# A gated linear recurrence and a SoLU feed-forward on one core: running sums in tiles of 32 columns, a ScalarE test in place of clamps, a carried phase on 16 rows, and a newly written order

## The chip, the core and the metric

The kernel runs on one core of a Trainium2 chip. The metric is the device time of one execution in microseconds. The engines are TensorE (PE; its weight loads are listed apart as PEld), VectorE (DVE), ScalarE (ACT), GpSimd (POOL) and SyncE (SP, which issues nearly all DMAs here).

## The reference, cut to what matters

For each of 4 batches and 8 heads a 48x48 complex state is decayed channel by channel and updated over 768 steps. The output of this part is the input of a feed-forward with 384 inputs and 1024 hidden units, over 3072 tokens.

```python
mag = np.sqrt(a_re * a_re + a_im * a_im)
scale = np.minimum(mag, 0.999) / (mag + 1e-06)
a_re_n, a_im_n = (a_re * scale, a_im * scale)
for t in range(S):
    new_re = ar * S_re - ai * S_im              # ar, ai: a_re_n, a_im_n at step t
    new_im = ar * S_im + ai * S_re
    S_re, S_im = (new_re + k_t v_t^T, new_im)
    y[t] = q_t @ S_re
x = y as (tokens, heads * 48)
h = x @ w_in
solu = h * softmax(h)
ln = (solu - mean) / sqrt(var + 1e-6) * g_ln
out = ln @ w_out
```

The weights arrive as 64-bit floats and are made into 32-bit ones on the chip. The other inputs have 32 bits.

## The kernel before, in words

A chunk is 128 steps of one batch: 24 chunks, numbered 4 x (block of time) + batch. Two chunks of neighbouring batches make a group, so there are 12 groups of 16 rows of heads (2 batches x 8 heads), each 128 x 768 numbers for one input. The recurrence inside a chunk becomes a masked product: the logarithms of the sizes and the angles of `a` are summed along time, and q and k are scaled and turned by the exponentials of these sums.

The steps of a group g, by name and engine:

- `load_ar`, `load_ai`, `load_q`, `load_k`, `load_v`, `load_vr` (SP): inputs. `load_vr` is four DMAs.
- `clamp` (DVE, L751 and L753): bounds both parts of `a`; the first instruction also leaves a maximum in `seen`.
- `inverse` (ACT): 1 / a_re as exp(-ln). `ratio` (DVE, two instructions): a_im / a_re, and a_re times the inverse, the start of a Newton step. `tangent` (DVE, L767 and the clamp L768): the corrected quotient.
- `square`, `secant`, `fourth`, `eps` (ACT), `size` and `lnm` (DVE, L781 and L788): the logarithm of the size with the reference's bound and its 1e-6. `fourth` (L777) leaves a sum in `seen`.
- `total0`, `total1` (PE, L793): a product with a triangular 128x128 matrix, the running sum over time, one chunk each. `grow`, `decay` (ACT): its exponentials. `trig`, `exp` (ACT): loads of a table of functions.
- `angle` (ACT, L833): arctangent. `on` (DVE, L838): adds the angle that the group two before left behind to row 0 of the tile. `phase0`, `phase1` (PE, L847): the running sum of the angles. `nearest` (ACT), `part` (DVE, then ACT), `cos`, `sin` (ACT): reduces the angle to a turn and takes the functions. `onward` (SP): copies the last row of angles for the next block of time, as one row of 768.
- `last` (SP, L804): the last row of the decays, as 16 rows of 48. `ends` (DVE, L818 and L819, and a POOL copy that doubles it): tests it. `turn_ends` (PE, L826), a transpose, and `tot` (DVE, L830): puts it on 96 partitions.
- `qs`, `ks` (DVE): scale q and k.

The steps of a chunk c: `k2`, `q2` (DVE, L906) turn k and q; `kqb` (DVE, L915) and `kqt0` (four DMAs, L920) transpose both; the first two chunks do it with `kt`, `qt` (PE) and `kT`, `qT` (ACT). `score0`, `score1` (PE, L962), `mask` (DVE), `values` (PE, L994) give y. `carry` (PE, L1002, tile f_d) and `add` (DVE) bring the state on. Then the feed-forward: `turned_x` (ACT), `up0`, `up1` (PE, L1035), `exp0` (ACT), `solu` (DVE), `blocks` (DVE) and `away` (four DMAs, to tile f_zT), `centred` and `norm` (POOL), `spread` (ACT), `down0`, `down1` (PE, L1112, tile f_o), `scale` (ACT), `store` (SP).

Weights come in 14 pieces: `fetch` (SP), `raised` (ACT, L692 and L694), `convert` (DVE). `mean`, `meansum`, `centre` fold the layer's mean into w_out. Each piece is fetched a second time (`again`) only to be tested (`inspect`, DVE). `verdict` counts all tests at the end; where one fails, a second, general kernel does the work over.

Most PE work is done in tiles of 128 rows by 32 columns of weights: four instructions with neighbouring column blocks make one product of 128 x 128. Only `total`, `phase`, `turn_ends` and the transposes of the first and last chunks use the full width.

Nothing is reordered by a scheduler: each engine, SP's DMA queue included, does its steps in the order in which they are written out. That order is given as text. `START` holds the first groups, `EVEN` and `ODD` repeat for the chunks 2 to 19, `END` holds the rest. Tiles rotate in small pools: PSUM tiles of the kind used for `total`, `phase` and `turn_ends` have two buffers, the tile of `kqb` one.

Of the kernel before, what the change touches and what calls it, by code (L numbers as in the profile page):

```python
# [504 lines left out]
WIDE = 1e10  # L505
# [9 lines left out]
START = """  # L515
load_ar:0 load_ai:0 clampb:0 clampa:0 inverseb:0 fetch:5 ratiob:0 inversea:0 raised:5 tangentb:0 ratioa:0
tangenta:0 fetch:9 squareb:0 raised:9 secantb:0 squarea:0 fourthb:0 sizeb:0 secanta:0 convert:9 fetch:0 epsb:0
sizea:0 fetch:13 lnmb:0 epsa:0 lnma:0 raised:0 fourtha:0 convert:0 convert:5 gain:0 fetch:2 total1:0 decay1:0
total0:0 grow1:0 load_q:0 load_k:0 decay0:0 grow0:0 qs1:0 trig:0 load_ai:1 anglea:0 raised:13 last:0 qs0:0
fetch:11 phase0:0 load_ar:1 fetch:4 angleb:0 ks0:0 nearest0:0 phase1:0 convert:13 fetch:1 ks1:0 load_vr:0  # L520
raised:2 part0:0 fetch:3 ends:0 nearest1:0 cosa:0 sina:0 convert:2 part1:0 k2:0 clamp:1 raised:11 cosb:0 q2:0
kt0:0 qt0:0 kT0:0 load_v:0 sinb:0 exp:0 qT0:0 fetch:8 kt1:0 k2:1 convert:11 inverse:1 kT1:0 fetch:7 turn_ends:0
q2:1 qt1:0 raised:4 ratio:1 tot:0 qT1:0 tangent:1 score1:0 kt0:1 convert:4 score0:0 mask0:0 raised:1 carry:1
add:1 fetch:12 raised:3 qt0:1 convert:1 kT0:1 square:1 convert:3 qT0:1 values:0 fetch:6 secant:1 fourth:1 kt1:1
qt1:1 turned_x:0 up0:0 raised:8 load_vr:1 kT1:1 raised:6 size:1 up1:0 eps:1 onward:0 raised:12 load_ai:2
convert:6 qT1:1 score1:1 convert:8 lnm:1 raised:7 convert:12 exp0:0 load_k:1 total0:1 grow0:1 total1:1 load_q:1
decay0:1 fetch:10 load_ar:2 decay1:1 grow1:1 convert:7 trig:1 solu0:0 qs1:1 angle:1 score0:1 raised:10 phase1:1
phase0:1 mask0:1 ks0:1 convert:10 nearest1:1 nearest0:1 carry:0 part1:1 part0:1 mean:0 add:0 clamp:2 centred:0
onward:1 mean:3 mean:4 cos:1 sin:1 last:1 qs0:1 mean:7 mean:2 mean:6 mean:1 load_v:1 k2:2 mean:5 meansum:0 q2:2
centre:5 kqb:2 load_v:2 kqt0:2 centre:7 exp:1 values:1 inverse:2 zt0:0 ratio:2 centre:0 zt1:0 tangent:2 centre:3  # L530
turned_x:1 up0:1 zT0:0 up1:1 centre:2 score0:2 centre:1 square:2 centre:4 score1:2 secant:2 centre:6 size:2
ks1:1 down0:0 zT1:0 fourth:2 load_q:2 mask0:2 ends:1 turn_ends:1 eps:2 lnm:2 values:2 load_vr:3 load_ar:3 tot:1
spread:0 k2:3 total0:2 load_k:2 exp0:1 norm:0 turned_x:2 total1:2 down1:0 decay1:2 decay0:2 q2:3 grow1:2 solu0:1
grow0:2 zt0:1 load_ai:3 kqb:3 kqt0:3 trig:2 zt1:1 qs1:2 angle:2 centred:1 on:2 zT1:1 again:0 ks1:2 ks0:2 up0:2
scale:0 zT0:1 phase1:2 phase0:2 nearest1:2 nearest0:2 part1:2 carry:2 part0:2 up1:2 clamp:3 cos:2 load_k:3
last:2 sin:2 qs0:2 exp:2 add:2 k2:4 store:0 exp0:2 spread:1 score1:3 score0:3 inverse:3 mask0:3 load_vr:2 q2:4
norm:1 down0:1 values:3 solu0:2 down1:1 zt1:2 kqb:4 load_k:4 kqt0:4 zt0:2 centred:2 turned_x:3 zT1:2 zT0:2
carry:3 spread:2 ratio:3 up0:3
"""
EVEN = """  # L540
tangent:g2 k2:3 scale:-1 square:g2 up1:1 score0:2 q2:3 secant:g2 load_ar:g3 again:-4 score1:2 down0:0 size:g2
kqb:3 eps:g2 spread:0 exp0:1 lnm:g2 norm:0 inspect:-5 total1:g2 load_q:g2 add:1 solu0:1 onward:g1 fourth:g2
decay1:g2 total0:g2 mask0:2 kqt0:3 grow1:g2 ends:g1 grow0:g2 down1:0 decay0:g2 inspect:-6 trig:g2 values:2
blocks:1 qs0:g2 score1:3 angle:g2 load_ai:g3 turn_ends:g1 on:g2 tot:g1 ks0:g2 turned_x:2 score0:3 phase0:g2
centred:1 phase1:g2 again:-3 clamp:g3 carry:2 up0:2 store:-1 nearest0:g2 nearest1:g2 last:g2 ks1:g2 part1:g2
part0:g2 add:2 cos:g2 sin:g2 load_vr:g2 away:1 mask0:3 load_k:g4 exp:g2 scale:0
"""
ODD = """
up1:1 k2:3 values:2 down0:0 load_v:g2 q2:3 kqb:3 qs1:g2 inverse:g3 exp0:1 store:-1 spread:0 solu0:1 turned_x:2
down1:0 kqt0:3 blocks:1 carry:2 norm:0 ratio:g3 away:1 up0:2 centred:1  # L550
"""
END = """
score0:22 scale:19 k2:23 score1:22 down0:20 up1:21 down1:20 q2:23 kqb:23 mask0:22 exp0:21 solu0:21 store:19
centred:21 spread:20 norm:20 kqt0:23 values:22 score1:23 turned_x:22 blocks:21 scale:20 score0:23 up0:22
mask0:23 spread:21 up1:22 norm:21 values:23 away:21 turned_x:23 down0:21 down1:21 exp0:22 solu0:22 ends:11
up0:23 store:20 up1:23 centred:22 blocks:22 scale:21 away:22 exp0:23 solu0:23 spread:22 down0:22 norm:22
centred:23 down1:22 zt0:23 zt1:23 scale:22 store:22 zT0:23 spread:23 zT1:23 store:21 down0:23 down1:23 norm:23
scale:23 store:23
"""


# [8 lines left out]
def whole(ctx, tc, flag, q, k, v, a_re, a_im, moe_w_in, moe_w_out, moe_g_ln, out):  # L570
# [170 lines left out]
    def prep_steps(g):  # L741
# [3 lines left out]
        def clamp(cs, o=g):  # L745
            if "lr" not in st:
                for nm in ("lr", "x0", "u"):
                    st[nm] = tmp.tile([P, GW], FP, tag=nm, name=f"f_{nm}")
# [509 lines left out]
```

## Time and profile before

| | |
|---|---|
| three timed runs | 437.94 us median (437.31 to 439.02) |
| the profiled execution | span 438.4 us, own time 441.15 us |
| instructions | 15186 |
| HBM read, written | 38.87 MB, 4.72 MB |
| all DMA | 72.52 MB in 167771 packets, mean 165 GB/s |
| granted TensorE clock, mean | 0.978 |

The profile is one execution recorded by the hardware. A line of a group says: line of the program, engine, operation, tile written <- tiles read, how often; then busy time and the mean of one. A line of the chain of waits has a start, a length and what ran, for the chain of work that ended last. A line of a timeline has a start, a length, engine, line, operation, shapes. Tile names have an f_ in front: f_L and f_phase are the running sums, f_o the result of down, f_h that of up, f_y that of values, f_d that of carry. A matmul of 32-bit numbers shows as two records.

### The profile page before, as it was taken

How to read it: one execution, taken by the hardware profiler on the slowest of the kernel's cores; microseconds unless marked ns; L12 is line 12 of the kernel's file. 1: busy time of each engine (PE TensorE's matmuls, PEld its weight loads, DVE VectorE, ACT ScalarE, POOL GpSimd, SP SyncE). 2: the span in 40 equal slices, each digit the busy share in tenths (PEclk: the TensorE clock that was granted, in tenths of full speed). 3: DMA queues.
4: the chain of work that ended last, by engine and by line, in shares of the span. 5: the costliest groups of instructions: out<-in, count | busy, mean ns of one | idle time of the engine just before them, and what ended most of it. 6: DMA issues, size and time to landing. Idle time of an engine off the chain costs nothing.

```text
span 438.4 us, 15186 instructions
## 1 busy us (share of the span) xinstructions
PE 392.0 (89%) x6590; PEld 220.2 (50%) x6590; DVE 361.2 (82%) x540; ACT 287.2 (65%) x453; POOL 51.7 (12%) x149
## 2 busy tenths in 40 slices
PE   0247858999999989999999999999999999999983
PEld 0025333555655545555554554654655646446861
DVE  4798899989889799799899899899899899753230
ACT  3998995986585685585576667668657757703160
POOL 3000011203001100101011011011021021102010
PEclk9985989999999999999999999999999999999999
DMA  8895808678758868989888878789879674473210
GB/s 222 203 261 160 188 9 184 122 180 179 171 113 192 202 145 200 210 175 221 202 187 203 196 181 207 168 206 223 190 177 204 166 157 107 111 191 85 47 38 29
DMA packets 167771, 72.52 MB, mean 165 GB/s; under 512 B 142224, under 2 KB 155536, under 8 KB 167696
## 3 DMA queue, kind: packets, MB, share of 16 engines
q1 hardware_dynamic: 167552, 71.14, 70.5%
q8 instruction: 54, 0.88, 0.9%
q10 hardware_dynamic: 144, 0.33, 0.3%
q14 instruction: 21, 0.17, 0.1%
HBM read 38.87 MB, written 4.72 MB: 99 GB/s over the span
## 4 chain that ended last, share of the span: by engine, by line
PE 73%; DVE 8%; ACT 8%; DMA 5%; issue 3%; SPq 2%; DVEq 0%
PE f_o L1112 26%; PE f_h L1035 22%; PE f_y L994 8%; PE f_score L962 6%; PE f_phase L847 3%; PE f_L L793 3%; PE f_d L1002 3%; DMA f_kqT<-f_kb 3%; DMA f_raw<-in_moe_w_in_dram 2%; SPq L920 1%; ACT f_bits L692 1%; DVE f_kb L915 1%; ACT f_bits L694 1%; DVE f_z L1054 1%; ACT f_kqT L933 1%
## 5 line engine op out<-in xcount | busy, mean ns | idle before, releaser
L1112 PE MATMUL f_o<-f_w_out,f_zT 128*32 128x384 f32 (+1 forms) x1344 | 132.9, 487 | 0.2 <-ACT f_zT L1067 0.2
L1035 PE MATMUL f_h<-f_w_in,f_xT 128*32 128x512 f32 x1152 | 130.4, 593 | 1.1 <-ACT f_xT L1028 1.1
L1112 PEld LDWEIGHTS f_o<-f_w_out,f_zT 128*32 128x32 f32 (+1 forms) x1344 | 60.8, 113 | 56.1 <-issue 46.0
L1035 PEld LDWEIGHTS f_h<-f_w_in,f_xT 128*32 128x32 f32 x1152 | 46.0, 110 | 63.9 <-issue 58.3
L915 DVE STREAM_TRANSPOSE f_kb<-f_kq 128x1536 f32<-128x1536 f32 x22 | 54.3, 2469 | 2.3 <-DMA f_kqT<-f_kb 2.0
L1054 DVE SCALAR_TENSOR_TENSOR f_z<-f_h,f_z 128x1024 f32<-128x1024 f32 (+1 forms) x36 | 33.9, 978 | 22.7 <-ACT f_z L1045 22.7
L1099 POOL TENSOR_SCALAR f_s<-f_s,f_sum 128x1 f32<-128x1 f32 x24 | 8.3, 348 | 272.2 <-ACT f_z L1093 272.1
L962 PEld LDWEIGHTS f_score<-f_kqT 96*32 96x32 f32 x1536 | 33.0, 112 | 14.5 <-issue 9.9
L1116 ACT ACTIVATE f_ot<-f_o,f_rs 128x384 f32<-128x384 f32 x24 | 14.0, 582 | 39.1 <-issue 18.2
L962 PE MATMUL f_score<-f_kqT 96*32 96x64 f32 (+3 forms) x1536 | 35.5, 239 | 4.4 <-DMA f_kqT<-f_kb 1.9
L1045 ACT ACTIVATE f_z<-f_h 128x1024 f32<-128x1024 f32 x24 | 29.3, 1219 | 13.6 <-PE f_h L1035 13.5
L994 PE MATMUL f_y<-f_att,f_vr 128*32 128x128 f32 x384 | 37.0, 273 | 0.0
L994 PE MATMUL f_y<-f_att,f_v 128*32 128x128 f32 (+1 forms) x384 | 36.6, 273 | 0.0
L793 PE MATMUL f_L<-f_lr,f_mats 128*128 128x384 f32 x48 | 20.0, 541 | 17.3 <-DVE f_lr L788 17.3
L994 PE MATMUL f_y<-f_kqT,f_state 96*32 96x128 f32 (+1 forms) x640 | 34.1, 272 | 0.0
L966 DVE TENSOR_TENSOR f_att<-f_score,f_mats 128x1024 f32<-128x1024 f32 x24 | 29.2, 1216 | 2.4 <-PE f_score L962 2.2
L994 PEld LDWEIGHTS f_y<-f_att,f_v 128*32 128x32 f32 (+1 forms) x384 | 22.6, 103 | 10.4 <-issue 7.7
L1093 ACT ACTIVATE f_z<-f_z,f_less 128x1024 f32<-128x1024 f32 x24 | 27.4, 1142 | 0.0
L847 PE MATMUL f_phase<-f_x,f_mats 128*128 128x384 f32 x48 | 20.5, 549 | 6.8 <-ACT f_x L833 6.8
L850 ACT ACTIVATE f_f<-f_phase,f_bias 128x384 f32<-128x384 f32 x24 | 13.9, 579 | 19.4 <-PE f_phase L847 18.5
L1072 DVE STREAM_TRANSPOSE f_zb<-f_z 128x1024 f32<-128x1024 f32 x20 | 24.7, 1236 | 0.3
L906 DVE TENSOR_TENSOR f_kq<-f_cs,f_k 128x768 f32<-128x768 f32 x24 | 22.8, 952 | 2.0 <-ACT f_cs L864 1.2
(104 smaller groups left out, 616.7 us busy)
## 6 DMA issues: line engine op xcount, KB each, us to landing
f_kqT<-f_kb SPq DMA_DIRECT2D x88, 192.0 KB, 3.4
f_zT<-f_zb SPq DMA_DIRECT2D x80, 128.0 KB, 3.2
f_raw<-in_moe_w_in_dram SPq DMA_DIRECT2D x12, 512.0 KB, 6.0
f_raw<-in_moe_w_out_dram SPq DMA_DIRECT2D x16, 384.0 KB, 5.6
f_ar<-in_a_re_dram SPq DMA_DIRECT2D x12, 384.0 KB, 4.8
f_ai<-in_a_im_dram SPq DMA_DIRECT2D x12, 384.0 KB, 4.9
f_q<-in_q_dram SPq DMA_DIRECT2D x12, 384.0 KB, 5.2
f_k<-in_k_dram SPq DMA_DIRECT2D x12, 384.0 KB, 5.1
```

Source lines behind the costliest of these rows:

```text
L793: nc.tensor.matmul(out=ps, lhsT=tri, rhs=st["lr"][:, i * DM:(i + 1) * DM], start=True, stop=True)
L847: nc.tensor.matmul(out=ps, lhsT=turns, rhs=st["x0"][:, i * DM:(i + 1) * DM], start=True, stop=True)
L915: nc.vector.transpose(out=t, in_=T["kq", c].rearrange("p n h (f j) -> p j (n h) f", j=3))
L962: nc.tensor.matmul(out=scores[r0:r0 + 32, x, r:], lhsT=QK[:, r // 32, x], rhs=QK[:, r // 32:, H + x], start=True, stop=True)
L966: nc.vector.tensor_tensor(out=st["att"].rearrange("p (i u) t -> p i u t", u=2), in0=scores.rearrange("p (i u) t -> p i u t", u=2), in1=mat ...
L994: nc.tensor.matmul(**product)
L1035: nc.tensor.matmul(out=st["h"][r:r + 32, half * 512:(half + 1) * 512], lhsT=st["xT"][:, c * P + r:c * P + r + 32], rhs=w_in[:, c, half * 5 ...
L1045: nc.scalar.activation(out=z, in_=h, func=AF.Exp, accum_out=sums[:, n:n + 1])
L1054: nc.vector.scalar_tensor_tensor(out=z, in0=h, scalar=1.0, in1=z, op0=OP.mult, op1=OP.mult, accum_out=st["sum"][:, 2 + i:3 + i])
L1072: nc.vector.transpose(out=st["zb"], in_=st["z"].rearrange("p (c s f) -> p s c f", s=4, f=32))
L1093: nc.scalar.activation(out=st["z"], in_=st["z"], func=AF.Square, bias=st["less"], accum_out=st["sum"][:, 1:2])
L1112: nc.tensor.matmul(out=st["o"][rows], lhsT=zT, rhs=w_out[:, c], start=(c == 0), stop=(c == KF - 1))
```

## The change

Five things are changed at once.

1. Running sums. `total` and `phase` go in four pieces of 32 columns of the triangular matrix. `turn_ends` goes in three products with the identity.

```diff
+        def running(ps, i, weights, nm):
+            for r in range(0, P, 32):
+                nc.tensor.matmul(out=ps[r:r + 32], lhsT=weights[:, r:r + 32], rhs=st[nm][:, i * DM:(i + 1) * DM],
+                                 start=True, stop=True)
...
-            nc.tensor.matmul(out=ps, lhsT=tri, rhs=st["lr"][:, i * DM:(i + 1) * DM], start=True, stop=True)
+            running(ps, i, tri, "lr")
...
-            nc.tensor.matmul(out=ps, lhsT=turns, rhs=st["x0"][:, i * DM:(i + 1) * DM], start=True, stop=True)
+            running(ps, i, turns, "x0")
...
-            nc.tensor.transpose(out=ps[0:D2], in_=st["e2"].rearrange("p u d -> p (u d)"), identity=ident[0:GH, 0:GH])
+            ends = rows[:, g].rearrange("p u d -> p (u d)")
+            for r in range(0, D2, 32):
+                nc.tensor.matmul(out=ps[r:r + 32, 0:GH], lhsT=ends[:, r:r + 32], rhs=ident[0:GH, 0:GH], start=True, stop=True)
```

2. The clamps of `a` and of the tangent are gone. A new step `sure` on ScalarE sums the squares of (a_re times its inverse, minus 1); the verdict tests that sum against `SURE`.

```diff
-            nc.vector.tensor_scalar(out=ar, in0=ar, scalar1=LEAST, scalar2=None, op0=OP.max, op1=OP.max,
-                                    accum_out=seen[:, 1, o:o + 1])
-            nc.vector.tensor_scalar(out=ai, in0=ai, scalar1=1e15, scalar2=-1e15, op0=OP.min, op1=OP.max)
...
+        def sure(cs, o=g):
+            nc.scalar.activation(out=st["u"][:, cs], in_=st["x0"][:, cs], func=AF.Square, bias=mone,
+                                 accum_out=seen[:, 1, o:o + 1])
...
-            nc.vector.tensor_scalar(out=x0, in0=x0, scalar1=1.5, scalar2=-1.5, op0=OP.min, op1=OP.max)
```

3. The ends. `last` writes the row once or twice (where the state goes on) into one tile for all groups; the step `ends` and its POOL copy are gone, one test of all rows stands in the verdict. `tot` moves to ScalarE.

```diff
-            st["ends"] = sml.tile([GH, D], FP, tag="ends", name="f_ends")
-            nc.sync.dma_start(out=st["ends"], in_=st["ar"][P - 1:P, :])
+            for u in range(2 if ti < NC - 1 else 1):
+                nc.sync.dma_start(out=rows[:, g, u], in_=st["ar"][P - 1:P, :])
...
-            nc.vector.tensor_copy(out=T["tot", g], in_=st["tot"][0:D2])
+            nc.scalar.copy(out=T["tot", g], in_=st["tot"][0:D2])
```

4. The carried phase. Row 0 of the angles is brought to 16 rows of 48 by a DMA (`first`), `on` adds there, and a second DMA (`back`) puts it in place before `phase`. `onward` writes 16 rows too.

```diff
-            x0 = st["x0"][0:1]
-            nc.vector.scalar_tensor_tensor(out=x0, in0=T["on", g - B // GB], scalar=2.0 * math.pi, in1=x0, op0=OP.mult,
-                                           op1=OP.add)
+            nc.vector.scalar_tensor_tensor(out=st["row"], in0=T["on", g - B // GB], scalar=2.0 * math.pi, in1=st["row"],
+                                           op0=OP.mult, op1=OP.add)
+        def first():
+            st["row"] = sml.tile([GH, D], FP, tag="first", name="f_first")
+            nc.sync.dma_start(out=st["row"], in_=st["x0"][0:1])
+        def back():
+            nc.sync.dma_start(out=st["x0"][0:1], in_=st["row"])
```

5. `raised` is one ScalarE instruction instead of two, and one text `ORDER` names every step of every group and chunk. The other edits only move where a tile is taken from its pool.

```diff
-            nc.scalar.activation(out=y.bitcast(FP), in_=T["raw", i][:, :, 0].bitcast(U32), func=AF.Identity,
-                                 scale=2.0 ** -29, bias=magic)
-            nc.scalar.activation(out=y, in_=y.bitcast(FP), func=AF.Identity, bias=mmagic)
+            nc.scalar.activation(out=y, in_=T["raw", i][:, :, 0].bitcast(U32), func=AF.Copy, scale=2.0 ** -29)
```

From the new order, the steps of PE, DVE, ACT and SP from the phase of group 6 to that of group 7 (each engine's list in its order):

```
PE  phase0:6 phase1:6 up0:10 values:11 up1:10 down0:9 carry:11 down1:9 up0:11 up1:11 score1:12 total1:7 total0:7
    score0:12 turn_ends:6 down0:10 down1:10 values:12 score0:13 score1:13 carry:12 phase0:7
DVE ks0:6 qs1:6 part0:6 part1:6 add:10 q2:12 k2:12 kqb:12 ratio:7 solu0:10 tangent:7 k2:13 blocks:10 q2:13 size:7
    kqb:13 lnm:7 solu0:11 add:11 mask0:12 blocks:11 on:7 qs0:7 ks1:7 mask0:13
ACT spread:9 nearest0:6 nearest1:6 sin:6 cos:6 exp:6 scale:8 inverse:7 exp0:10 turned_x:11 sure:7 square:7 secant:7
    fourth:7 scale:9 eps:7 exp0:11 grow1:7 decay1:7 grow0:7 decay0:7 trig:7 angle:7 spread:11 turned_x:12 tot:6 spread:10
SP  store:6 load_ar:7 away:9 load_ai:8 onward:6 load_k:7 kqt0:12 away:10 kqt0:13 load_vr:7 first:7 load_q:9 last:7
    store:9 back:7 load_v:8
```

The same stretch in the order before:

```
PE  phase0:6 phase1:6 carry:10 up0:10 up1:10 values:11 down0:9 down1:9 carry:11 up0:11 up1:11 score0:12 score1:12
    down0:10 total1:7 total0:7 down1:10 values:12 score1:13 turn_ends:6 score0:13
DVE clamp:7 ks1:6 part1:6 part0:6 add:10 mask0:11 k2:12 q2:12 kqb:12 qs1:6 solu0:10 blocks:10 ratio:7 tangent:7 k2:13
    q2:13 size:7 kqb:13 lnm:7 inspect:5 add:11 solu0:11 mask0:12 ends:6 inspect:4 blocks:11 qs0:7 on:7 ks0:7
```

Of the second fetches of the weights, six stand in the new order ahead of the phase of group 2, two between those of the groups 2 and 9, and six behind; before, one stood ahead of the phase of group 2, one behind that of group 10, and the rest in between, two to a group.

## The prediction

> **What bounds the kernel now.** I read the page first, for each engine's load and how it lies over the span (40 slices of 10.96 us).
>
> ```profile
> PE 392.0 (89%) x6590; PEld 220.2 (50%) x6590; DVE 361.2 (82%) x540; ACT 287.2 (65%) x453; POOL 51.7 (12%) x149
> PE   0247858999999989999999999999999999999983
> ```
>
> TensorE does little for some 60 us and is then busy almost to the end. The busy time by stretch, cut where the first phase matmul of a group (two chunks) starts, says more (columns: stretch, length, then PE, PEld, DVE, ACT, POOL busy, clock, DMA share, GB/s):
>
> ```profile
> 0.00:23.20 23.20, 2.94 (x5) 1.05 (x5) 14.81 (x39) 15.92 (x30) 3.91 (x12) 1.00 0.82 202
> 23.20:59.55 36.35, 23.45 (x297) 13.55 (x297) 32.87 (x62) 33.76 (x56) 0.85 (x4) 0.81 0.71 185
> 59.55:88.64 29.09, 26.52 (x308) 13.38 (x308) 28.44 (x49) 22.58 (x35) 4.89 (x9) 0.94 0.58 119
> 88.64:120.72 32.08, 31.05 (x510) 18.79 (x506) 28.15 (x44) 22.65 (x34) 4.77 (x13) 1.00 0.81 181
> 216.34:247.61 31.27, 31.27 (x590) 17.22 (x586) 29.39 (x41) 21.20 (x33) 3.35 (x11) 1.00 0.88 202
> 372.42:438.40 65.98, 57.75 (x800) 35.93 (x798) 24.79 (x42) 22.51 (x36) 7.53 (x25) 0.98 0.34 84
> ```
>
> Second row: ACT and DVE are full, PE is not. Third: DVE is full. From the fourth on PE is the bound, 31.27 us a group, with DVE only 6% behind. The chain of waits names the pieces of one such group:
>
> ```profile
> 206.41 2.58 PE f_o L1112 x32
> 208.99 1.49 PE f_L L793 x4
> 210.48 2.72 PE f_o L1112 x32
> ...
> 216.34 1.51 PE f_phase L847 x4
> 217.85 0.77 PE f_d L1002 x45
> ...
> 230.74 0.64 PE f_d L1002 x45
> ```
>
> The same 32 f_o instructions take 2.58 us after tiled work and 2.72 behind the full-width f_L; f_d takes 0.64 and, behind the full-width f_phase, 0.77. So going back to tiles costs 0.14 and 0.13 us. VectorE's timeline, in the same group:
>
> ```profile
> 221.82 0.96 DVE L906 TENSOR_TENSOR f_kq<-f_cs,f_k 128x768 f32<-128x768 f32 x1
> 231.99 0.56 DVE L768 TENSOR_SCALAR f_x<-f_x 128x768 f32<-128x768 f32 x1
> 237.73 0.91 DVE L788 SCALAR_TENSOR_TENSOR f_lr<-f_lr,f_u 128x768 f32<-128x768 f32 x1
> 245.03 0.95 DVE L838 SCALAR_TENSOR_TENSOR f_x<-f_on,f_x 1x768 f32<-1x768 f32 x1
> ```
>
> From the first phase matmul (216.29) to the end of lnm (238.64) it is 22.35 us, nearly all DVE work in a row; L793 starts at 240.19, 1.55 us later. So today the sum is ready before PE wants it. The row L838 stands right behind the arctangent (244.15 to 244.99): no DMA between them.
>
> **Running sums in pieces.** A piece has the shape of an f_o instruction, 128*32 128x384, and 64 of those take 5.16 us, so four pieces in two passes take 5.16/8 = 0.645 us. A group now pays 1.49 + 0.14 + 1.51 + 0.13 = 3.27 us and will pay 4 x 0.645 = 2.58: 0.69 less, 8.3 us over 12 groups. The two half scores with the full-width transpose of the carried totals between them take 1.38 us (end of f_y at 277.50 to f_phase at 278.88), without it 1.14, so it costs 0.24; six tiny tiled matmuls at f_d's pace (0.64/48 = 13 ns each) cost 0.1. That is 0.14 x 10 = 1.4 us. PE work falls by 9.7 us and its floor for a group is 30.4.
>
> **Clamps and checks.** DVE loses L751 (0.95 with its read), L753 (0.48), L768 (0.48), ends (0.32), the tot copy (0.17), and on falls from 0.95 to about 0.17 (16x48 rows, as L818 takes 0.167): 3.2 us a group. ACT gains sure, priced by L777, which is also a Square with an accumulated sum (0.74 and 0.19 us), and tot (0.2): 21.2 to 22.4 of 30.4, not a bound. sure sits ahead of square, which must wait for tangent anyway, and tangent stands behind solu on DVE: that covers it; uncovered it would be 0.9 us a group.
>
> **Start.** One of two ACT passes over each weight piece goes: 4.9 + 4.3 us over 14 (L694). Ten of them lie in the second stretch: ACT there loses 10 x 0.66 and gains 1.1, DVE loses clamp:1 (1.43), the tangent clamp, ends and tot, 2.4 in all. ACT falls to 28.3 and DVE to 30.5 of 36.35; since DVE is next, the stretch shrinks by 2.4 to 5.5, I take 3.5. The first stretch is a chain: two clamps and three second passes go (about 2.5), two sure with reads come (1.4): 1.0. Start: -4.5 us.
>
> **The new order and the two new transfers.** This decides the steady part. In the new order PE has, between phase0 and the next total, 2 phases (1.29), 4 half ups (10.28), 2 half downs (5.16), values (1.76), carry (0.64) and a half score (0.57): 19.7 us. It now moves both last half downs behind total. lnm must be ready by then. The old 22.35 us lose L768 (0.48), a qs that goes into the wait for the cosine (0.43), and about 0.9 more: 0.5 because part0 no longer queues behind both nearest and phase is shorter (k2 now starts 5.53 us after phase0), 0.4 because DVE neighbours that depend on each other are parted (solu to blocks now takes 1.35 us, 1.14 elsewhere). That leaves 20.6 us. So PE reaches total 0.9 us early and waits. After total it has 2 totals (1.29), 2 downs (5.16), values, carry, turn_ends and three half scores (1.71): 10.66 us until phase0. Cycle: 20.6 + 10.66 = 31.3 us, what it is now. The 0.83 us of PE work that is saved turns into a wait for lnm. In about half the groups two spreads (1.14 + 0.19 each) stand between turned_x and nearest on ACT and may push nearest by up to 0.65. From both sides a cycle lies between the floor 30.4 and 32.0; I take 31.3.
>
> The carried phase now goes angle, first (DMA), on, back (DMA), phase. Measured from total, angle ends at 4.7 us (now 240.19 to 244.99, less 0.1); with issue hops and on (0.17) the row is back at 5.2 + d1 + d2, d being a landing time. PE wants it at 10.66, so the two may take 5.4 us together. The nearest row is the fetch of the last row, 3 KB:
>
> ```profile
> L804 SPq DMA_DIRECT2D f_ends<-f_ar x12: 545/549/3737, 20.9 to 368.0; - x12
> DMA to landing us min/median/max: 1.6/3.7/6.1
> ```
>
> Bounds for the pair: 3.2 (both like the quiet one at 368.0, issued 5.1 us after a kqt0 and a store began) and 7.4 (both at the median, each behind 384 to 512 KB loads). In the new order first comes some 5.6 us after kqt0 began and usually nothing big after it, so d1 is near 1.6 to 2.5; back follows a q load and a store of 576 KB together, so 2 to 2.5. I take 4.5: hidden, 0.9 us to spare. A repeat of the median costs 2.0 us a cycle. The Trainium skill ("DMA: Bandwidth & Descriptors", Anatomy of one DMA) states about 2.0 us of fixed cost a DMA, mostly the write receipt, and so speaks against putting two in a chain; by it the pair would be an estimated 4.0 us and still hidden, and here the trace's own 1.6 is below it and its median far above. Queued behind these waits: on DVE behind on stand qs, ks and mask (values needs mask 3.9 us after phase0 starts); on SP behind first a q load and stores, behind back the v and ar loads and away, whose zT is wanted 8.2 us after phase0; on ACT behind tot stand spread and nearest.
>
> **Sum.** The profiled execution has a span of 438.4 and its own time is 441.15; the three timed runs have a median of 437.94, so I take a change of span as the change of the median. Start -4.5. Third and fourth stretch: PE has 25.2 + 31.2 instead of 26.0 + 29.2 us by new prices, and in the third lnm (it ended 20.8 us after phase0:1, less a tangent clamp: 20.3) plus 10.4 of PE work behind total makes 30.7 instead of 29.1; fourth 31.9 instead of 32.1: +1.4. Eight cycles to phase0:11: 8 x 31.3 = 250.4 instead of 251.7: -1.3 (the old ones hold one of 33.10). Tail: PE-bound, one phase chunk belongs before the mark: -1.0. Together -5.4, so 437.9 - 5.4 = 432.5.
>
> **The rivals.** (1) PE keeps the bound. If lnm is ready at 19.7 (DVE at 84% has room), cycles are 30.4: 0.9 x 9 = 8 less, 424. For it: DVE loses 3.2 us a group. Against: those ops mostly stood in waits, not in the 22.35. Chance 0.2, between 418 and 427. (2) On the slower side: back lands late. At medians phase waits 2.0 us in each of 9 cycles: +18, 450. It decides from d1 + d2 over 5.4. For it: 3.3 to 5.0 us landings in the loop; against: two re-fetches of weights a group (about 0.9 MB of 6) mostly leave this part of the order. Chance 0.25, between 440 and 458. (3) The change doesn't do what it says: the sum of squares passes SURE and the flag starts the other kernel. No row here prices that; it would be far outside. Chance 0.02. My forecast, wait for lnm and hidden transfers, has 0.53, between 426 and 440.
>
> **Numbers.** About 0.5% is what this kernel's runs can tell from no change (437.31 to 439.02). Faster by more (under 435.75): 0.2 and four fifths of 0.53, 0.63. Same: 0.10. Slower: 0.27. The range 419 to 448 leaves out part of rival 2, the third, and the edge of rival 1.
>
> **What would show it.** Pieces at 0.645 us a chunk and no longer f_o or f_d behind them; PE idle before total, ended by lnm, about 0.9 us a group; none before phase. Idle before phase ended by the DMA that writes f_x shows rival 2; PE without idle time and cycles of 30.4 rival 1. phase0:1 should start near 55. If it starts at 59 or later, the start is not bound by ACT and DVE work and that term is wrong.

## The result and the profile after

The changed kernel takes 451.85 us (median of four runs, 449.68 to 454.21), the one before 437.62 beside it: a ratio of 1.032, with a 95% interval of 1.026 to 1.039. The prediction was 432.5 with a range of 419 to 448, so it was wrong in sign and size. The profiled execution has a span of 449.1 us and took 450.93.

The page, engine loads and TensorE's 40 slices (now 11.23 us each):

```profile
PE 389.8 (87%) x6928; PEld 210.4 (47%) x6928; DVE 327.0 (73%) x457; ACT 290.3 (65%) x475; POOL 47.2 (11%) x139
PE   0259668999999997998999899998999899999993
```

VectorE lost 34 us of work and TensorE 2, and the span grew by 10.7: less work didn't mean less time. The busy time by stretch, cut again at the first phase matmul of a group:

```profile
0.00:22.19 22.19, 2.79 (x16) 0.55 (x16) 13.13 (x34) 14.82 (x31) 3.48 (x11) 1.00 0.97 230
22.19:52.83 30.64, 20.18 (x279) 10.86 (x279) 28.26 (x52) 27.87 (x49) 0.71 (x2) 0.88 1.03 228
52.83:86.80 33.97, 27.55 (x440) 14.49 (x444) 26.69 (x42) 23.35 (x37) 2.58 (x10) 0.91 0.86 185
86.80:119.98 33.18, 32.16 (x536) 18.04 (x530) 25.39 (x36) 24.76 (x40) 6.95 (x15) 1.00 0.75 148
152.44:187.91 35.47, 32.48 (x612) 16.42 (x615) 24.43 (x31) 21.56 (x37) 2.21 (x8) 0.95 0.74 161
221.36:254.72 33.36, 31.07 (x633) 16.83 (x623) 26.35 (x32) 23.41 (x38) 6.43 (x17) 1.00 0.77 169
354.38:384.59 30.21, 29.93 (x564) 17.45 (x568) 25.70 (x32) 21.90 (x34) 5.18 (x12) 1.00 0.57 132
```

Against before: phase 0 of group 1 starts 6.7 us earlier (52.83, 59.55). The stretch to the phase of group 2 is 4.9 longer (33.97, 29.09). The nine cycles from there to the phase of group 11 are 14.0 longer (297.8 in all, 283.7; a mean of 33.1, 31.5). What follows is 1.5 shorter (64.6, 66.1). Sum: +10.7, the whole change of the span. In the loop VectorE is at 69 to 85% of these stretches. Only the last cycle, 30.21, is nearly all TensorE work (29.93); in the eight others TensorE is busy for 30.8 us or more. The nine cycles together, before and after:

```profile
88.64:372.42 283.78, 281.32 (x5189) 156.32 (x5185) 260.32 (x351) 192.39 (x298) 34.50 (x100) 1.00 0.81 184
86.80:384.59 297.79, 282.45 (x5396) 154.11 (x5391) 231.34 (x284) 203.01 (x326) 33.20 (x92) 0.99 0.73 158
```

TensorE is busy for about as long as before. Its pauses grew from 2.5 to 15.3 us, and that is most of the 14.0.

TensorE's waits between 86 and 385 us (columns: total, times, longest):

```profile
PE f_L L839 <- DVE f_lr L834: 9.4, 8, 2.3
PE f_d L1050 <- issue: 2.1, 3, 1.6
PE f_phase L839 <- DMA f_x<-f_first: 2.0, 1, 2.0
PE f_d L1050 <- ACT f_xT L1076: 1.4, 2, 0.7
```

The first is total waiting for lnm. Phase waited for back once (2.0). One cycle (152.44 to 187.91) shows how lnm gets late. VectorE's timeline, then SyncE's (start, length, line, what, in brackets the idle time before and what ended it):

```profile
159.18 2.42 DVE L964 STREAM_TRANSPOSE f_kb<-f_kq 128x1536 f32<-128x1536 f32 x1
169.50 0.95 DVE L827 SCALAR_TENSOR_TENSOR f_lr<-f_u,f_lr 128x768 f32<-128x768 f32 x1
172.41 2.28 DVE L964 STREAM_TRANSPOSE f_kb<-f_kq 128x1536 f32<-128x1536 f32 x1 [1.96 <-DMA f_kqT<-f_kb]
174.61 0.91 DVE L834 SCALAR_TENSOR_TENSOR f_lr<-f_lr,f_u 128x768 f32<-128x768 f32 x1
```

```profile
158.56 3.39 SPq L695 DMA_DIRECT2D f_ai<-in_a_im_dram  x1
162.05 1.50 SPq L917 DMA_DIRECT2D f_on<-f_f  x1
163.60 2.05 SPq L705 DMA_DIRECT2D f_vr<-in_v_dram  x4
165.76 2.64 SPq L969 DMA_DIRECT2D f_kqT<-f_kb  x4
```

The first kqb ended at 161.60. SyncE was still issuing a load of `a`, onward and four loads of v, and came to kqt0, which empties the one f_kb tile, at 165.76. The second kqb had to wait for that until 172.41, 1.96 us of them idle, and lnm stands behind it. In three of the nine cycles VectorE stands idle ahead of the second kqb (1.96, 2.52 and 1.83 us), and in these total waits longest for lnm: 2.3, 2.1 and 1.9 us, against 0.3 to 0.9 in five others. The chain of waits ends this in the same place:

```profile
172.83 1.12 ACT f_z L1093 x2
173.95 0.03 issue
173.98 0.02 DVEq L1102
174.00 0.61 issue
174.61 0.92 DVE f_lr L834
175.53 0.04 issue
175.58 2.79 PE f_L L839 x16
```

The last row is total for both chunks, 2.79 us where it takes 1.31 elsewhere: the granted clock halves behind the wait (stretches of 3.4 us; PE busy, clock, DMA share, GB/s):

```profile
171.80:175.20 3.40, 1.51 (x44) 1.00 0.71 225
175.20:178.60 3.40, 3.02 (x31) 0.50 0.71 163
```

The carried phase's two DMAs, first and back (third row: VectorE's idle time ahead of on, and how often; last row: landing of the two, min/median/max):

```profile
L886 SPq DMA_DIRECT2D f_first<-f_x x10: 529/549/1277, 79.5 to 379.4; - x10
L889 SPq DMA_DIRECT2D f_x<-f_first x10: 531/543/545, 84.8 to 381.4; - x10
  DMA f_first<-f_x: 6.9, 7
DMA to landing us min/median/max: 1.6/1.7/4.9
```

They land at least as quickly as was reckoned (1.7 us in the median; 4.5 was taken for the two together). But VectorE stood idle 6.9 us in all with on at the head of its queue and qs, ks and mask behind it.

### The profile page after: what moved, and what is told of

It is laid out like the page before. It is cut to its first block, busy times and chain, and to the rows that moved or that the text cites. A ratio compares the mean times of both kernels' runs of the same rounds, so it can differ in the third digit from the quotient of the medians.

```text
span 449.1 us, 15846 instructions
## 1 busy us (share of the span) xinstructions
PE 389.8 (87%) x6928; PEld 210.4 (47%) x6928; DVE 327.0 (73%) x457; ACT 290.3 (65%) x475; POOL 47.2 (11%) x139
## 4 chain that ended last, share of the span: by engine, by line
PE 48%; SPq 13%; DVE 11%; ACT 10%; issue 8%; DMA 7%; POOL 0%; DVEq 0%; ACTq 0%; POOLq 0%
PE f_o L1160 17%; PE f_h L1083 14%; PE f_y L1042 5%; PE f_L L839 4%; DMA f_kqT<-f_kb 3%; PE f_score L1009 3%; PE f_phase L839 3%; SPq L705 3%; DVE f_kq L955 2%; DMA f_ar<-in_a_re_dram 2%; SPq L1125 2%; SPq L1169 2%; PE f_d L1050 2%; DVE f_lr L834 2%; SPq L969 2%
## 5 line engine op out<-in xcount | busy, mean ns | idle before, releaser
L1083 PE MATMUL f_h<-f_w_in,f_xT 128*32 128x512 f32 x1152 | 132.3, 599 | 2.4 <-ACT f_xT L1076 2.1
L1160 PEld LDWEIGHTS f_o<-f_w_out,f_zT 128*32 128x32 f32 (+1 forms) x1344 | 58.3, 114 | 59.5 <-issue 43.3
L1083 PEld LDWEIGHTS f_h<-f_w_in,f_xT 128*32 128x32 f32 x1152 | 44.5, 111 | 71.0 <-issue 67.4
L839 PE MATMUL f_L<-f_lr,f_mats 128*32 128x384 f32 x192 | 22.0, 579 | 28.6 <-DVE f_lr L834 26.9
L1076 ACT COPY f_xT<-f_y 128x384 f32<-128x384 f32 x24 | 11.4, 473 | 43.4 <-PE f_y L1042 43.2
L1009 PE MATMUL f_score<-f_kqT 96*32 96x128 f32 (+3 forms) x1536 | 34.6, 236 | 0.3 <-DMA f_kqT<-f_kb 0.3
L1138 POOL TENSOR_SCALAR f_less<-f_sum 128x1 f32<-128x1 f32 x24 | 6.8, 294 | 196.3 <-DVE f_z L1102 196.0
L839 PE MATMUL f_phase<-f_x,f_mats 128*32 128x384 f32 x192 | 20.7, 547 | 7.6 <-ACT f_x L877 2.9
L955 DVE TENSOR_TENSOR f_kq<-f_cs,f_q 128x768 f32<-128x768 f32 x24 | 22.6, 944 | 6.0 <-ACT f_cs L910 6.0
```

Of the source, the lines that this page charges most:

```text
L839: nc.tensor.matmul(out=ps[r:r + 32], lhsT=weights[:, r:r + 32], rhs=st[nm][:, i * DM:(i + 1) * DM], start=True, stop=True)
L955: nc.vector.tensor_tensor(out=t, in0=T["cs", g][:, i * H:(i + 1) * H], in1=heads(T[nm, g][:, i]).unsqueeze(2).to_broadcast([P, H, 2, D]), ...
L1009: nc.tensor.matmul(out=scores[r0:r0 + 32, x, r:], lhsT=QK[:, r // 32, x], rhs=QK[:, r // 32:, H + x], start=True, stop=True)
L1083: nc.tensor.matmul(out=st["h"][r:r + 32, half * 512:(half + 1) * 512], lhsT=st["xT"][:, c * P + r:c * P + r + 32], rhs=w_in[:, c, half * 5 ...
L1160: nc.tensor.matmul(out=st["o"][rows], lhsT=zT, rhs=w_out[:, c], start=(c == 0), stop=(c == KF - 1))
```

## The experiments

"Cycles" are the nine from the phase of group 2 to that of group 11; their sum is 283.7 us before and 297.8 after. Ratios are to the kernel before, with the 95% interval.

Stretches are read from one execution each, and one of them varies much. The changed kernel, e1 and e18 are the same program up to the phase of group 2, and there the stretch from the phase of group 1 to that of group 2 took 33.97, 37.89 and 32.33 us. (TensorE's wait for kqt0 in it was 0.3, 1.9 and 0 us, the mean granted clock 0.91, 0.82 and 0.91.) So in the new order a difference of up to 5.6 us in this stretch alone tells nothing of an edit.

**First four: which part costs.**

e1: the changed kernel with lnm ahead of the second kqb in groups 3 to 11, in the order's text for group 7:

```diff
-size:7 ... up1:11 eps:7 kqb:13 exp0:11 lnm:7
+size:7 ... up1:11 eps:7 lnm:7 kqb:13 exp0:11
```

> The changed kernel with one step moved: in the groups 3 to 11 lnm stands on VectorE ahead of the second kqb of the group instead of behind it (and eps ahead of it in the text, where it wasn't). Theory A (the new order: the second kqb waits for its single buffer, that is for the kqt0 of the first chunk, and lnm and so total wait behind it): TensorE's waits for lnm between the groups 3 and 11, 9.5 us together, nearly go, the two stretches at half clock (3.4 us each) with them; 438 to 442 us. Theory B (the two transfers of the carried phase are what costs): the time stays within 2 us of 452, the wait turns up ahead of phase.

456.37 us, 1.043 (1.035 to 1.052). The wait for lnm is gone (0.6 us in all), and others have come:

```profile
PE f_phase L839 <- DMA f_x<-f_first: 6.6, 4, 3.7
PE f_d L1050 <- issue: 3.7, 4, 2.2
PE f_score L1009 <- DVE f_zb L1120: 1.3, 1, 1.3
```

Phase to total falls to 19.9 us in five groups, total to phase grows to 14.8 in two. The nine cycles take 298.8 us, 1.0 more than in the changed kernel: the wait moved to the other half of the cycle. Of the 5.9 us by which the span is longer, 3.9 lie ahead of the first moved step, in the stretch that varies.

e2: without the two row DMAs; on works in row 0 of the tile, as before, and GpSimd doubles the last row in place of a second DMA (of the edit, on is shown).

```diff
-            nc.vector.scalar_tensor_tensor(out=st["row"], in0=T["on", g - B // GB], scalar=2.0 * math.pi, in1=st["row"],
-                                           op0=OP.mult, op1=OP.add)
+            x0 = st["x0"][0:1]
+            nc.vector.scalar_tensor_tensor(out=x0, in0=T["on", g - B // GB], scalar=2.0 * math.pi, in1=x0, op0=OP.mult,
+                                           op1=OP.add)
```

> The changed kernel and its order without first and back: on adds to row 0 in place, as before the change, and the last row is doubled by a GpSimd copy instead of a second transfer. Theory A: only the one group whose phase waited for the transfer (2.0 us) and three issue slots a group on SP come back, 445 to 451 us. Theory B: the time before the change or less, 438 us or under.

448.9 us, 1.024 (1.017 to 1.032). Cycles 290.1, 7.7 less; the stretch to group 2 is 2.4 longer, which is within its spread, the end 2.1 longer. In these two executions the row DMAs cost 0.9 us a cycle although phase waits for them only once. Over the whole kernel the gain, 3 us, isn't clear of the noise.

e3: all parts but the row DMAs, in the order of before (sure right behind ratio).

> All parts of the change except the two transfers (on as before, rows doubled by GpSimd), but in the order before the change, sure put right behind ratio. Theory A: the parts are good and the order loses: PE work falls by 0.67 us a group, the start is a few us shorter, 425 to 432 us. If the parts themselves cost (sure and tot on ScalarE, the tests), it is 438 us or more.

448.72 us, 1.026 (1.019 to 1.033). Cycles 283.3: the loop's loss is gone. The time is not: the stretch to the phase of group 2 takes 36.06 us instead of 29.09. ScalarE's timeline there:

```profile
71.67 0.94 ACT L808 ACTIVATE f_u<-f_x,f_bias 128x768 f32<-128x768 f32 x1 [3.52 <-DVE f_x L805]
72.51 0.18 ACT L808 ACTIVATION_READ_ACCUMULATOR f_u<-f_x,f_bias 128x1 f32 x1
72.61 0.46 ACT L1077 COPY f_xT<-f_y 128x384 f32<-128x384 f32 x1
84.62 0.17 ACT L874 COPY f_tot<-f_tot 96x16 f32<-96x16 f32 x1 [5.50 <-PE f_tot L870]
85.83 2.02 ACT L1094 ACTIVATE f_z<-f_h 128x1024 f32<-128x1024 f32 x1
```

sure (first row) waits 3.52 us for ratio with the copy of y behind it, for which TensorE waits 5.0 us; tot (fourth row) waits 5.50 us with exp0 behind it.

e4: the kernel before with total and phase in four pieces, nothing else.

> The kernel before, with one edit: total and phase in four pieces of 32 columns. If TensorE bounds the middle: 0.67 us less in 12 groups, 429 to 431 us. If VectorE, 6% behind, takes over or the order before the change waits elsewhere: 433 to 438 us.

436.09 us, 0.995 (0.992 to 0.998); undisturbed cycles of 30.60 instead of 31.27.

**Next four: the start, sure and tot.**

e5: e4 and one ScalarE pass for each weight piece (the diff of `raised` above).

> The kernel before, with two parts of the change only: running sums in four pieces and one ScalarE pass over each weight piece instead of two; its order, clamps and the carried phase are those of before. Theory A (the shorter start of the changed kernel comes from the second ScalarE passes, and what is lost between the phase of group 1 and that of group 2 comes from sure and tot on ScalarE): the phase of group 1 starts at 56 to 57.5 instead of 59.32 with pieces alone, the next group takes 30 us as with pieces alone (29.83), the time is 433 to 434.5. Theory B (a shorter start brings the next group's work ahead of its inputs and weights, whatever stands on ScalarE): the phase of group 1 comes as early, but the next group takes 32 us or more and the time stays at 436.

433.29 us (eight runs, 430.79 to 436.55), 0.990 (0.986 to 0.994). The phase of group 1 starts at 56.12 instead of 59.32 and the stretch after it keeps 30.03. Theory A. This is the fastest version of all that were run.

e6: e3 with tot on VectorE.

```diff
-            nc.scalar.copy(out=T["tot", g], in_=st["tot"][0:D2])
+            nc.vector.tensor_copy(out=T["tot", g], in_=st["tot"][0:D2])
```

> The changed kernel in the old order and without the two row DMAs (448.72 us), with tot back on VectorE. Theory A (a waiting tot on ScalarE holds up what is queued behind it; there tot of group 1 waited 5.50 us for its product): from the phase of group 1 to that of group 2 it takes 33 to 34 us instead of 36.06, the cycles of the loop stay at 31.4, the time is 446 to 447. Theory B (tot costs nothing, sure alone does it): 36 us and 448 to 449.

446.07 us, 1.018 (1.011 to 1.024); the stretch to group 2 takes 37.23. With sure in place tot doesn't decide: ScalarE waits 3.9 us for ratio there, as in e3, and TensorE 3.7 us for the copy of y.

e7: e3 without sure.

```diff
-        chain = dict(inverse=inverse, ratio=ratio, sure=sure, tangent=tangent, square=square, secant=secant,
+        chain = dict(inverse=inverse, ratio=ratio, tangent=tangent, square=square, secant=secant,
```

> The changed kernel in the old order and without the two row DMAs, with the step sure left out (so the test on a_re times its inverse is not made). Theory A (sure of group 2 waits 3.52 us on ScalarE for ratio and holds up turned_x, for which TensorE then waits 5.0 us and runs at half clock for 6.8): the stretch from the phase of group 1 to that of group 2 takes 31 to 32 us instead of 36.06, the cycles 31.0 instead of 31.4 since tangent no longer waits for ScalarE, the time is 441 to 443. Theory B (tot does it, sure is hidden): 35 to 36 us, 448.

436.80 us, 0.997 (0.994 to 1.000), 12 less than e3. By span it is 8.0 less: 2.0 in the first stretch, 1.4 in the second, 2.7 in the third, 1.6 at the end, and 0.3 in the nine cycles (283.0, 283.3). TensorE's wait for the copy of y in the third stretch, 5.0 us in e3, is 0.5. So sure is hidden in the loop and not in the start. What is left there is tot:

```profile
78.54 0.17 ACT L873 COPY f_tot<-f_tot 96x16 f32<-96x16 f32 x1 [3.39 <-PE f_tot L869]
```

e8: the changed kernel in its new order with the row DMAs, without sure, tot on VectorE (both edits above).

> The changed kernel in its new order with both row DMAs, without the step sure (so that test is not made) and with tot back on VectorE. Theory A (the two new ScalarE steps hold up others): the stretch to the phase of group 2 takes 31 us instead of 33.97; TensorE waits for lnm 5 us in the loop instead of 9.4, since tangent follows ratio directly; cycles 32.5 instead of 33.1; the time is 442 to 445. Theory B (the new order and the two row DMAs cost what they cost without these steps: lnm stands behind the second kqb, which waits for the transposing DMA, and mask, qs and ks behind on): cycles stay at 33 and the time at 447 to 451.

456.16 us, 1.042 (1.035 to 1.049): no faster than with both. By the medians it is 4 us slower, but the two intervals overlap. Neither theory expected that.

```profile
PE f_L L838 <- DVE f_lr L833: 10.3, 7, 2.8
PE f_phase L838 <- DMA f_x<-f_first: 4.4, 3, 2.2
```

The waits for lnm are as long as in the changed kernel, so sure does not cause them, and phase waits three times for back.

**Then four: the new order itself.**

e9: e2 with one half down ahead of total in groups 3 to 11, as before. In groups 4 to 6 its transfer away goes ahead of lnm too.

```diff
-lnm:7 score1:12 total1:7 ... turn_ends:6 down0:10 down1:10
+lnm:7 score1:12 down0:10 total1:7 ... turn_ends:6 down1:10
```

> The changed kernel without the two row DMAs (448.9 us), in its new order, with one of the two half downs that the new order puts behind total moved ahead of total again, in the groups 3 to 11. Theory A (the new order asks for lnm 2.6 to 5 us earlier than VectorE has it, and that wait with the refill and the half clock behind it is what the loop loses): the waits of total for lnm (6.8 us in the loop) fall under 1.5, the cycles from the phase of group 2 to that of group 11 from a mean of 32.0 to 31.0, the time is 439 to 443. Theory B (something else in the new order holds the loop, and a wait that is taken away turns up before another instruction, as with lnm moved ahead): cycles of 31.8 to 32.2 and 447 to 450, with new waits before down, score or phase.

448.32 us, 1.021 (1.014 to 1.028). Total no longer waits for lnm, and the cycles of groups 4 to 6 are at 30.87, 31.39 and 31.70. In the next two (33.07 and 34.03) the half down, 2.58 us of work, takes 4.7 and 4.9:

```profile
PE f_o L1161 <- DMA f_zT<-f_zb: 2.0, 3, 1.0
```

Its transfer away stands too late in the order there. The first cycle takes 35.88 us, with other waits (1.3 us for the state, 1.9 ahead of f_d), and the nine take 292.0, 1.9 more than in e2. So theory A holds for three cycles, theory B for the sum.

e10: e2 with lnm ahead of the second kqb (e1's move).

> The changed kernel without the two row DMAs, with lnm ahead of the second kqb on VectorE in the groups 3 to 11. With the row DMAs that move took the wait for lnm away and made the time longer (456.37 us), waits before phase and before the state's product growing. Theory A (the row DMAs and what is queued behind on made it longer): without them cycles are 31.0 to 31.4 and the time 440 to 444. Theory B (the second kqb and its transposing DMAs, now later, come too late for the scores): cycles of 32 or more, 448 to 453, with waits before score or values.

449.51 us, 1.022 (1.018 to 1.027), the same as e2; theory B in its time. So without the row DMAs too, taking the wait for lnm away gains nothing. Whether the row DMAs are why e1 is slower than the changed kernel stays open: those two intervals overlap.

e11: the old order with both row DMAs and without sure.

```diff
 angle:7
+first:7
 ... on:7
+back:7
```

> The changed kernel in the old order, with the two row DMAs (first right behind angle, back right behind on) and without sure (so that test is not made); without the row DMAs this is 436.80 us. Theory A (the pair takes 4 to 5 us and the old order leaves 7.1 us from total to phase, of which the arctangent takes 4.7): phase waits 2.5 to 3.5 us in each of nine cycles, cycles of 34 to 35, 465 to 475 with the half clock behind such waits; so the new order was what the row DMAs need. Theory B (they are hidden in either order): cycles of 31.5, 437 to 440.

484.02 us, 1.104 (1.100 to 1.108), 47 more than e7, cycles of 35.5:

```profile
PE f_phase L838 <- DMA f_x<-f_first: 30.6, 9, 6.5
```

In the old order, total to phase is 7.1 us, and phase waits 3.4 us a cycle for back. The new order is what makes room for the row DMAs: it puts total 2.7 us earlier in the cycle (21.4 us behind phase, 24.0 before), and there lnm isn't ready.

e12: pieces, one pass, rows of the decays in one tile, tot on VectorE, no row DMAs; the new order with sure up to phase 0 of group 1, then the old order with the clamps, each written right ahead of inverse.

> A version put together from what gained: running sums in pieces, one pass over each weight piece, the row of the decays straight into one tile, tot on VectorE, the carried phase as before; up to phase 0 of group 1 the new order with sure in place of the clamps (groups 0 and 1), from there the old order with the clamps. Theory A (the start's gain and the old loop add up): the phase of group 1 at 52.5 instead of 56.1 with one pass alone, 30 to 31 us to that of group 2, cycles of 31.0, 428 to 431 us. Theory B (the work and the loads that the earlier start leaves behind come back in the next group): 33 us or more to the phase of group 2 and 433 us, as with one pass alone.

463.26 us, 1.055 (1.051 to 1.059), cycles of 32.9 to 35.3. Both theories missed: it was the place of the clamps. Phase to total takes 26.0 us instead of 23.6. Moving 1.4 us of VectorE work within its own queue, off the wait and onto the path, cost 2.4 us there, and 2.1 a cycle on the mean of the nine (303.2 us; 284.1 in e13).

**Last six, on what was still open.**

e13: e12 with the clamps where the kernel before has them.

> The version with the new start and the old loop again, but with each clamp where the kernel before has it, at the beginning of the cycle, and not right ahead of inverse, where the last version had put it (cycles of 33.1 to 34.3 and 463.26 us: 26.0 us from phase to total instead of 23.6). Theory A (that place of the clamps made the path from phase to lnm 2.5 us longer): cycles of 30.6 to 31.5 again, 30 to 33 us from the phase of group 1 (52.9) to that of group 2, 429 to 434 us. Theory B (the new start leaves work behind that the old loop can't take up): the phase of group 2 at 88 or later, 437 us or more.

439.85 us, 1.002 (0.999 to 1.006); cycles 284.1, as before. The phase of group 1 comes at 52.80 and that of group 2 at 87.62, later than e5's 86.15, which started its group 1 3.3 us later. The early start gains nothing here, and the kernel is 6.6 us slower than e5.

e14: e2 with every kqt0 from chunk 4 on right behind its kqb on SyncE.

```diff
-kqb:12 ... load_ai:8 ... onward:6 ... load_k:7 ... kqt0:12
+kqb:12 kqt0:12 ... load_ai:8 ... onward:6 ... load_k:7
```

> The changed kernel without the two row DMAs (448.9 us), with the transposing DMAs kqt0 of every chunk from 4 on issued right behind kqb on SyncE instead of behind loads, weights and stores. Theory A (lnm is late because the second kqb waits for the first one's transfer to free the one buffer, 6.9 us in the changed kernel): the waits of VectorE for that transfer go, total waits under 3 us in the loop instead of 6.8, cycles 31.3, 442 to 445. Theory B (lnm is late by VectorE's own work, at 20.2 against 19.7 us of TensorE's work, in every group): the waits for lnm stay at 5 us or more and the time at 447 to 450.

493.38 us, 1.123 (1.116 to 1.130).

```profile
PE f_o L1161 <- DMA f_zT<-f_zb: 30.5, 6, 6.4
PE f_L L838 <- DVE f_lr L833: 2.8, 7, 0.9
```

The wait for lnm falls from 6.8 to 2.8 us, but at most 0.6 of that for theory A's reason: in e2 VectorE hardly waited for its f_kb tile. Of e2:

```profile
PE f_L L838 <- DVE f_lr L833: 6.8, 7, 1.6
DVE f_kb L965 <- DMA f_kqT<-f_kb: 0.6, 1, 0.6
```

There lnm is late by other work and waits of VectorE, and why it comes earlier in e14 isn't shown. SyncE now stands idle until kqb is done (15.2 us in one cycle, 158.79 to 174.04):

```profile
157.29 1.50 SPq L694 DMA_DIRECT2D f_ar<-in_a_re_dram  x1
174.04 2.68 SPq L970 DMA_DIRECT2D f_kqT<-f_kb  x4
```

It comes to its loads and to away that much later, and TensorE waits 30.5 us for away.

e15: e9 with each away right behind blocks.

> The last version with a half down ahead of total, and now with each away issued right behind blocks, since that half down had waited for away's transfer in the groups where away stands late in the written order (cycles 33.07 and 34.03; 30.87 and 31.39 elsewhere). Theory A (the new order's loop loses only what total waits for lnm): cycles from group 3 on of 30.7 to 31.3, 443 to 446, the rest of the difference to before lying ahead of the phase of group 3. Theory B: waits turn up elsewhere again, cycles of 32, 448.

487.41 us, 1.110 (1.103 to 1.117): the same in reverse, 18.4 us of waits of score for kqt0 and 14.3 for the copy of y.

e16: e7 with tot on VectorE.

> The changed kernel in the old order, without the two row DMAs, without sure (so that test is not made) and with tot on VectorE; with tot on ScalarE it is 436.80 us. Theory A (a tot that waits on ScalarE, 3.4 us there, holds up exp0 and with it VectorE's solu, 3.9 us, between the phases of the groups 1 and 2): that stretch takes 30 us instead of 33.4, 431 to 434 us. Theory B (the stretch is as long because the start became shorter; the phase of group 2 can't come before 86 us): 33 us, 436 to 438.

436.19 us, 0.994 (0.991 to 0.998). The stretch to group 2 is 29.94 instead of 33.40, but it starts 1.4 us later; the phase of group 2 comes at 85.81 instead of 87.83. ScalarE's wait for tot's product, 3.4 us, and VectorE's for the exp0 behind it, 3.9, are gone. The whole kernel is no faster than e7, whose interval overlaps. (Its profiled execution is the longest of ten, 440.14, so only this stretch is read.)

e17 and e18: kqt0 of the first chunk of each group (6, 8 ... 22) alone right behind its kqb, without and with the row DMAs.

> The changed kernel without the two row DMAs (448.9 us), with kqt0 of each group's first chunk alone (6, 8, ... 22) issued on SyncE right behind its kqb, ahead of four to seven loads; kqt0 of the second chunks and away stay where they are. Theory A (the second kqb waits for that transfer, which stands behind loads that SyncE issues first, and lnm stands behind the second kqb): VectorE no longer waits for it, phase to total takes 20.2 us in every group instead of up to 21.6, total waits 3 us in the loop instead of 6.8, cycles of 31.4 instead of 32.2, 444 to 446 us. Theory B (as in three earlier moves, the wait turns up elsewhere): 447 to 452.

> The same move in the changed kernel itself, with both row DMAs (451.85 us). Theory A (late lnm and the row DMAs are separate costs that add): phase to total 20.2 us in every group instead of up to 23.1, total waits 3 us in the loop instead of 9.4, cycles of 32.3 instead of 33.1, 444 to 448 us, 1 to 3 above the run without the row DMAs. Theory B (the wait moves to phase, behind back, as when lnm was put first): 450 to 457.

1.061 (1.051 to 1.070; 460.82 to 469.71 us) and 1.069 (1.063 to 1.075; 460.04 to 469.10 us): both theories missed. Of e18:

```profile
PE f_o L1160 <- DMA f_zT<-f_zb: 6.3, 6, 2.1
PE f_o L1160 <- ACT f_x L877: 3.4, 1, 3.4
PE f_L L839 <- DVE f_lr L834: 2.2, 7, 0.8
```

VectorE's waits for its f_kb tile are gone, and total's wait for lnm falls from 9.4 to 2.2 us. So that is where the large lnm waits of the changed kernel came from. The time is lost elsewhere (the nine cycles take 308.7 us): SyncE stood idle for 5.1 us (226.87 to 231.97) in one cycle with kqt0 at its head, two loads, onward and away behind it.

## Why the prediction was wrong

**Pieces: right.** 1.29 and 1.31 us for a pair of chunks (2 x 0.645). In the old order an undisturbed cycle falls by 0.67 us where 0.69 was reckoned, since TensorE bounds it there; the nine cycles fall by 4.0, the kernel by 0.5%.

**Clamps and checks: sizes right, worth nothing.** VectorE lost 34 us. In e7, without clamps and without sure, the cycles stay at the pieces' level or above (283.0 against 279.7): the VectorE work that left had stood in its waits. "That covers it" held for sure in the loop, not in the start, where the price of 0.9 us a group became 6.1 us of the first three stretches, of 8.0 us of span in all (e3 and e7; the runs differ by 12). A waiting sure holds what is queued behind it on ScalarE.

**Start: right in kind, short in its second half.** 6.7 us instead of 4.5; the passes alone give 3.2 (e5). But the sum let the third and fourth stretch give back 1.4 us, and they gave back 6.0, 4.9 of it in the third (by the same measure 3.2 in e18 and 8.8 in e1, whose instructions there are the same). In this execution the term failed by 4.6 us. The work of TensorE behind total was priced; the waits were not. In the changed kernel's trace they are waits of TensorE for ScalarE's copies in the third stretch: 2.7 us of phase for tot's, 2.1 of up and 1.7 of total for others. The first two are as long in e1 and e18. The prediction named what is queued behind tot and gave it no price. How much of the 4.6 us they are isn't shown: with tot back on VectorE its waits are gone (e7 and e16), but the time stays, and the stretch by itself varies by 5.6.

**The cycle: the step that failed.** "20.6 + 10.66 = 31.3" measured 21.4 + 11.7 = 33.1 (means of nine): 0.8 us too little for lnm, 1.1 for the way back to phase. The sum has two kinds of time in it, 30.4 us of TensorE work and 0.9 of waiting for lnm; the nine cycles would be 273.6 us of work and 8.1 of waits. Measured were 282.4 and 15.3. The wait for lnm itself came to 9.4 us, near 8.1, and that is luck: it was to be 0.9 in every group from VectorE's work, and it was 0.3 to 0.9 in five, with 6.3 of the 9.4 in the three that waited for f_kb, a wait that the prediction put at nothing. The other waits of TensorE, 5.8 us, were put at nothing too (2.0 for back, 1.4 for the copy of y, 2.4 without a shown cause). Of the 8.8 us by which the work is longer, 3.2 are half clock; for the rest no run names a cause. In the best groups the first half is what was reckoned (20.24 and 20.29). The step let every step's wait be the same in all groups, and the upper end of 32.0 allowed for one nudge only, of nearest. It left out three things that the runs show. SyncE issues one DMA after another: the lengths of its rows add up to 224 us in the 298 us of the nine cycles (229 of 284 before), so kqt0 or away come several us late when anything ahead of them waits (shown by the SyncE rows, by e14 and e18 for kqt0, by e9 and e15 for away). Two of the four waits of 1.9 us or more were followed by 3.4 us of half clock, which cost 1.5 and 1.7 us. And on at the head of VectorE's queue held mask and the scalings (6.9 us in all); without the row DMAs the nine cycles are 7.7 us shorter.

**The row DMAs: right in time, wrong in cost.** "Hidden, 0.9 us to spare" held for phase in eight cycles of nine. The section that the prediction cites for 2.0 us a DMA gives that figure for DMAs that GpSimd issues; SyncE issues these, and they landed in 1.6 us at the least. The old order couldn't have hidden them (e11). So the new order paid for them with an earlier total, and what they save on VectorE, 0.95 us down to 0.2, is not on the path in either.

**The rivals.** Rival 2 said 450 us, near what was measured, for a reason that gave 2.0 us of its 18: phase waited for back once. That its number is near is luck. Rival 1, TensorE as the bound, is what undisturbed cycles are with pieces alone in the old order (30.60; 31.08 on the mean of nine).

**Still open.** Why e8, with less on ScalarE, is no faster than the changed kernel. And why the stretch to the phase of group 2 differs so much from one execution to the next: with the same instructions that phase came at 85.20, 86.80 and 90.86 us (e18, the changed kernel, e1). Both look like waits trading places, but no run takes that apart.

## What to carry to other kernels

In an order written by hand for queues that work strictly in order, price a moved step by what stands behind it on each queue, SyncE's issue queue too, and not by its own length. Room that is made for a slow step comes out of some other step's slack: look up that step's spread over all groups, not its best group. Work taken off an engine that has pauses gains nothing unless something on the path waits for that work. Before a stretch is compared between two runs, look how much it varies with the same instructions. Here two parts that shortened TensorE's and ScalarE's own work (433.29 us) beat all five together by 18.6 us.

## What the runs showed of the hardware

Issuing is not free. One transposing DMA takes SyncE 0.61 us to issue and lands in 3.5 us (medians). The Trainium skill ("DMA: Bandwidth & Descriptors", Issuing engines are not separate DMA queues) calls the time that a sequencer takes to initiate a DMA usually small relative to the DMA itself, and for one DMA these rows agree. But the rows follow one another: four transposing DMAs take 2.6 to 3.5 us to issue, as long as one takes to land, and SyncE's rows fill three quarters or more of the loop (224 of 298 us).

TensorE need not be idle for its clock to fall: behind a stretch of 3.4 us with 1.51 us of matmuls in it, the granted clock was 0.50 for the next 3.4 us. Two other waits as long (2.1 and 2.0 us) were not followed by that. The Trainium skill ("TensorE: Matmul & The Clock Gate", What's actually happening) speaks of an idle window of about 3.4 us; the length agrees, the idleness was only 56% here.
